# Interleaving v's rows of four heads over all partitions, and turning k behind the value products, in a chunked-attention and mixture-of-experts kernel

## The chip, the cores and the metric

The kernel runs on one core of a Trainium2 chip. The metric is the device time of one execution in microseconds (us), as the median of several runs. The core has a matrix engine (PE, with its weight loads PEld), a vector engine (DVE), a scalar engine (ACT), a general engine (POOL) and a queue engine (SP). POOL, ACT and SP also issue transfers (DMAs). Each engine works through its own instructions strictly in program order, and engines wait for each other through semaphores.

## What is computed

```python
# attention: 4 batches, 8 heads, 768 rows, 64 columns; 8 memory rows a head
for c in range(24):                       # chunks of 32 rows
    k_ctx = k[:, :, max(0, 32*c - 16):min(768, 32*c + 40)]     # 16 left, 8 right; v_ctx the same
    scores = scale * q_c @ concat(mem_k, k_ctx).T
    a = exp(scores - max); a /= a.sum()
    out[:, :, chunk c] = a @ concat(mem_v, v_ctx)
# router: each of the 3072 rows x (512 columns) goes to its 2 best of 8 experts
noisy = x @ w_gate + log1p(exp(x @ w_noise)) * noise
out[row] = sum over the two experts of weight * (relu(x @ w1[e]) @ w2[e])
```

So a chunk's 32 queries see 56 context rows and 8 memory rows, 64 in all.

## The kernel before

**Stages.** First comes the attention with the router, then the experts. The attention is a loop of 16 iterations (L579 to L638). Iteration i works on "pair" i. Pairs 2g and 2g+1 are the two halves (12 chunks each) of group g, which holds four heads of one batch; there are eight groups, two to a batch. The experts' stage begins at L655. It gathers rows by pairs of experts and runs the two products of each expert (L752, L760).

**One iteration.** The order is written out by hand (`tc.manual_schedule`), so the program text gives each engine's order. In iteration i stand, in this order:

- `PT_pe(i-1)` (L311): six transposes on PE of the probabilities P of the pair before, and `PT_dve(i-1)` (L318) which copies them to SBUF (tile PT).
- `max_dve(i)` (L299): the maximum of the scores of pair i, on DVE.
- `qkT_pe(i+2)` (L246): twelve transposes of q and twelve of k on PE for two heads. ACT copies q (L256, tile qT).
- `kT_act(i+2)` (L260): ACT copies k from PSUM into the block-diagonal buffer `kd` (`kbufs`), in two halves (L264). Before, the first half stands ahead of P's exponential and the second behind it.
- `sub_dve(i)` (L304): DVE subtracts the maximum, and ACT takes the exponential into P (L308).
- `PV_pe(i-1)` (L323): the value products on PE, six with the memory rows (L329) and 24 with the context rows of v (L333), into the single buffer `ps_o`.
- `scores_pe(i+1)` (L269): scores of the next pair on PE into the single buffer `ps_s`: the memory part (L278), which needs only q, and the chunks (L288), which need k.
- `mult_dve(i-1)` (L337): DVE divides the value products by the sums (L345, L346) into the row tile `xrow`.
- `xT_pe(i-2)` (L351): PE transposes those rows for the router, and ACT copies them (L359, tile xt).

Scores of pairs 2g and 2g+1 both need q and k of both head pairs of group g. With q and k turned two iterations ahead, an odd iteration i turns heads that the scores of pair i+1 need at once, and an even one turns heads that are needed one iteration later.

**PSUM slots.** P's transposes, q's, k's, the rows' and the router's tiles share three slots in turn (pool `psT`, L90). A transpose waits until the slot's last reader is done.

**Values.** The four heads of a group share one weight matrix PT, so v's rows lie block by block: head hd has partitions 32 hd to 32 hd + 27 (28 partitions, two rows in each), the rest of the columns is zero. The four memory partitions of each head (32 hd + 28 to 32 hd + 31) are in `memv` (L180), which also has one column of ones a head for the sums. P is written in the same order (head, row) (L307). `memory_values` (L186) copies memory rows of `mv_nat` (L150) into `memv`, on POOL, for groups 0 and 1 before the loop and for the others in iteration 2.

**Loads.** q, k and v are loaded and cast by POOL's queue, q and k one transfer a group each (L112), v one a head (L120). v has three buffers: a load waits until the products of the group before in that buffer are done. POOL also clears buffers (L139), makes constants (L212), does part of the routing and issues the loads of the first expert weights in iteration 11.

**Routing.** After the last pair of a batch, `begin_route(b)` (L541) computes the batch's logits on PE and puts the steps of `route(b)` (L375) in a list. `early_steps` and `late_steps` (L552, L557) run one entry's first and second half in each iteration: best-of comparisons (`s1m` to `s2b`), the gates (`s4`, which also sends the batch's rows to DRAM on SP's queue), the counts (`s3`, `s5`, `s5b`, `s6`) and sums (`s7`, `s8`). The last batch's steps run after the loop.

## Time and profile before

| | us |
|---|---|
| median of three runs (lowest to highest) | 341.62 (340.74 to 343.32) |
| the profiled execution's own time | 341.32 |
| its span, first to last instruction | 339.6 |
| busy in the span: PE, DVE, ACT, POOL | 294.8, 167.0, 132.1, 141.0 |

The profile is of one execution. A row of the timeline gives the start in us from the span's start, the duration, the engine, the line of the program, the operation, the tile written and the tiles read, the shape, how many instructions are merged in the row, and in brackets the idle time before it with what ended it ("issue" where nothing the profile shows was waited for). A row of a table by stretches gives the stretch, its length, the busy time of the chosen instructions with their number, the granted clock of PE, the share of the transfer engines, and the rate in GB/s of bytes written. A row of waits gives who waited for what, the total in us, the number of waits and the longest. A row of groups has the number of instructions, then the busy time in us and the mean of one in ns, then the idle time before them.

### The profile page before, as it was taken

What the parts mean: (1) busy time and instruction counts of PE and PEld (TensorE: products, weight loads), DVE (VectorE), ACT (ScalarE), POOL (GpSimd) and SP (SyncE); (2) the same over time, 40 slices, a digit from 0 to 9 for tenths busy, and PEclk for the clock granted to TensorE, in tenths of its full rate; (3) what the DMA queues carried; (4) which work ended last, traced back from release to release, by engine and by line L of the source; (5) the groups of instructions that cost most, each with busy time, mean ns of one, the idle gap of its engine ahead of it and who ended that gap; (6) DMA issues with size and microseconds to landing.
All of it is one profiled execution on the core that took longest, in us unless ns stands there. A gap on an engine that the chain in (4) does not pass through costs nothing.

```text
span 339.6 us, 8160 instructions
## 1 busy us (share of the span) xinstructions
PE 294.8 (87%) x3492; PEld 179.7 (53%) x3492; DVE 167.0 (49%) x337; ACT 132.1 (39%) x232; POOL 141.0 (42%) x183
## 2 busy tenths in 40 slices
PE   1698897878853779999999999999999999999990
PEld 1576676666642555547547545545545545545530
DVE  7776788798877653223223233334414423433440
ACT  7877886786430323333333223313133113103100
POOL 8899986274333776400061043034250222131161
PEclk9999999999995699999999999999999999999997
DMA  7999999979991379970059029419759128121021
GB/s 101 183 187 200 184 162 181 226 73 206 200 259 47 96 106 225 215 156 2 2 92 235 16 66 201 86 55 166 164 118 198 48 80 135 40 87 50 29 107 66
DMA packets 58407, 42.87 MB, mean 126 GB/s; under 512 B 32215, under 2 KB 51799, under 8 KB 58368
## 3 DMA queue, kind: packets, MB, share of 16 engines
q0 software_dynamic: 49808, 38.80, 69.0%
q1 hardware_dynamic: 8272, 3.44, 4.7%
q8 instruction: 29, 0.48, 0.5%
q10 hardware_dynamic: 288, 0.07, 0.1%
q14 instruction: 10, 0.08, 0.1%
HBM read 61.32 MB, written 10.65 MB: 212 GB/s over the span
## 4 chain that ended last, share of the span: by engine, by line
PE 70%; DMA 7%; ACT 7%; DVE 6%; POOL 4%; issue 4%; POOLq 0%; DVEq 0%; ACTq 0%
PE ps_h L752 31%; PE ps_y L760 26%; DMA kg<-in_k_dram 4%; ACT kd L264 2%; PE ps_o L329 2%; PE ps_o L333 2%; ACT xt L359 2%; DMA wgn_f<-in_moe_w_noise_dram 2%; PE p_t L697 2%; POOL out_dram L768 1%; PE ps_s L288 1%; PE p_x L357 1%; PE ps_s L779 1%; ACT P L308 1%; ACT qT L256 1%
## 5 line engine op out<-in xcount | busy, mean ns | idle before, releaser
L752 PE MATMUL ps_h<-xTb,w1t 128*128 128x512 bf16 (+3 forms) x608 | 106.3, 324 | 2.0 <-DVE xTb L698 2.0
L760 PE MATMUL ps_y<-w2t,ht 128*128 128x512 bf16 x448 | 102.0, 379 | 0.0
L752 PEld LDWEIGHTS <-w1t 128*128 128x128 bf16 x864 | 63.9, 97 | 45.2 <-DVE xTb L698 1.6
L768 POOL DMA_INDIRECT out_dram<-acc,sidx x28 | 27.9, 996 | 139.2 <-DVE acc L767 134.4
L740 DVE TENSOR_SCALAR ht<-ps_h 128x416 bf16<-128x416 f32 (+2 forms) x64 | 40.0, 625 | 72.4 <-PE ps_h L752 72.4
L738 ACT ACTIVATE ht<-ps_h 128x416 bf16<-128x416 f32 (+2 forms) x72 | 37.9, 526 | 75.4 <-PE ps_h L752 71.1
L760 PEld LDWEIGHTS <-ht 128*128 128x128 bf16 x448 | 41.8, 97 | 46.7
L764 ACT ACTIVATE acc<-ps_y,meta 128x512 f32<-128x512 f32 x28 | 19.2, 687 | 69.3 <-PE ps_y L760 56.6
L752 PE MATMUL ps_h<-xTs,w1t 128*128 128x32 bf16 x256 | 45.4, 177 | 0.2 <-DVE xTs L713 0.2
L767 DVE SCALAR_TENSOR_TENSOR acc<-ps_y,meta,acc 128x512 f32<-128x512 f32 x28 | 21.0, 751 | 37.3 <-PE ps_y L760 35.7
L688 POOL DMA_INDIRECT xl<-x_rows,gidx x28 | 29.6, 1058 | 14.3 <-issue 4.6
L120 POOL DMA_DIRECT2D vg<-in_v_dram x34 | 25.3, 750 | 4.6 <-PE ps_s L293 2.2
L698 DVE COPY xTb<-p_t 128x512 bf16<-128x512 bf16 x28 | 11.6, 422 | 29.5 <-PE p_t L697 29.4
L264 ACT COPY kd<-p_t 64x768 bf16<-64x768 bf16 x32 | 25.3, 792 | 1.2 <-PE p_t L253 0.8
L359 ACT COPY xt<-p_x 128x768 bf16<-128x768 bf16 x16 | 12.8, 799 | 15.2 <-PE p_x L357 15.2
L329 PE MATMUL ps_o<-memv,PT 128*128 128x260 bf16 x96 | 14.2, 284 | 3.5 <-DVE xrow L346 1.8
L253 PE MATMUL p_t<-identb,qg 128*64 128x128 bf16 x192 | 9.9, 246 | 7.5 <-DMA qg<-in_q_dram 6.5
L301 DVE TENSOR_REDUCE mx<-ps_s 128x12 f32<-128x768 f32 x16 | 15.2, 948 | 2.1 <-PE ps_s L293 1.2
L346 DVE TENSOR_TENSOR xrow<-ps_o,rec 128x768 bf16<-128x768 f32 x16 | 15.3, 958 | 0.6
L306 DVE TENSOR_TENSOR sd<-ps_s,mx 128x768 f32<-128x768 f32 x16 | 15.2, 949 | 0.1
L308 ACT ACTIVATE P<-sd 128x768 bf16<-128x768 f32 x16 | 13.5, 844 | 3.3 <-DVE sd L306 3.2
L256 ACT COPY qT<-p_t 128x768 bf16<-128x768 bf16 x16 | 12.8, 798 | 4.1 <-PE p_t L253 3.9
(144 smaller groups left out, 304.4 us busy)
## 6 DMA issues: line engine op xcount, KB each, us to landing
w1t<-in_moe_w_dram POOLq DMA_DIRECT2D x8, 1024.0 KB, 11.6
w2t<-in_moe_w_dram POOLq DMA_DIRECT2D x8, 1024.0 KB, 9.9
vg<-in_v_dram POOLq DMA_DIRECT2D x30, 168.0 KB, 9.2
qg<-in_q_dram POOLq DMA_DIRECT2D x7, 384.0 KB, 8.3
kg<-in_k_dram POOLq DMA_DIRECT2D x7, 384.0 KB, 10.3
x_rows<-xrow SPq DMA_DIRECT2D x3, 792.0 KB
x_rows<-xrow SPq DMA_DIRECT2D x2, 384.0 KB
xl<-x_rows,gidx POOLq DMA_INDIRECT x28, 7.2
```

The costliest lines, as they stand in the source:

```text
L120: nc.gpsimd.dma_start(out=vg[p0 + j:p0 + j + nj, c:c + n, hd, :, :].rearrange("p c e d -> p c (e d)"), in_=bass.AP(v.tensor, v.offset + (g ...
L264: nc.scalar.copy(st[n]["kT"][hs, hh, :].rearrange("d (p j) -> d p j", j=SJ), st[n]["p_k"][hs].rearrange("d j p -> d p j"))
L329: nc.tensor.matmul(out=po[:, u, :OW], lhsT=PT[:, 2 * u + e, :], rhs=memv[:, g, e, :], start=(e == 0), stop=False, skip_group_check=True)
L359: nc.scalar.copy(xt, p_x)
L688: nc.gpsimd.indirect_dma_start(out=xl, out_offset=None, in_=xd, in_offset=bass.IndirectOffsetOnAxis(ap=gidx[:, p:p + 1], axis=0), bounds_c ...
L738: nc.scalar.activation(out=dst, in_=src, func=Act.Relu)
L740: nc.vector.tensor_scalar(out=dst, in0=src, scalar1=0.0, scalar2=None, op0=Alu.max)
L752: nc.tensor.matmul(out=ps_h[:, o:o + w], lhsT=w1t[:, kp, f * 128:(f + 1) * 128], rhs=rhs(kp), start=(kp == 0 and i == 0), stop=(kp == KP - ...
L760: nc.tensor.matmul(out=ps_y, lhsT=ht[:, f, j * CAP:(j + 1) * CAP], rhs=w2t[:, f, :], start=(f == 0), stop=(f == FB - 1))
L764: nc.scalar.activation(out=accs[acc[p]], in_=ps_y, func=Act.Copy, scale=gate)
L767: nc.vector.scalar_tensor_tensor(out=a, in0=ps_y, scalar=gate, in1=a, op0=Alu.mult, op1=Alu.add)
L768: nc.gpsimd.indirect_dma_start(out=out_part[p], out_offset=bass.IndirectOffsetOnAxis(ap=sidx[:, p:p + 1], axis=0), in_=a, in_offset=None, ...
```

## The change

It has three parts. First, the order of partitions in the value products: row j of head hd moves from partition 32 hd + j to 4 j + hd. v's loads write every fourth partition; P is written as (row, head) instead of (head, row), so that the exponential writes with a step of four elements. Memory rows now lie in partitions 112 to 127. Because the four heads alternate there, `memory_values` no longer copies blocks: it multiplies the memory rows by a column `lane` that is 1 in the partitions of one head and 0 in the others. `lane` is made of an iota on POOL and two operations on DVE, and a third spreads it into the ones columns of `memv` in place of four memsets.

Second, the place of k: `qkT_pe` is called for q alone where it stood, and k's transposes with both of ACT's copies stand behind the value products, directly ahead of the next scores.

Third, the end of the loop: in the last iteration the scaling of pair 14 and the sending of its rows are moved up, the routing steps of batch 2 are divided anew, and after the loop the transposes of pair 14's rows stand before the last value products.

```diff
@@ -95,6 +95,7 @@
         groups = {}
 
         NVB, NKB = 3, 4
+        HB = 2 * GP
         turn_of = [0, 1, 0, 2, 1, 0, 2, 1]
         vbufs = [ap_.tile([128, ncnk, 2 * GP, 2, D], BF16, name=f"vg{i}", bufs=1) for i in range(NVB)]
         kbufs = [ap_.tile([128, 2, S], BF16, name=f"kd{i}", bufs=1) for i in range(NKB)]
@@ -114,11 +115,11 @@
         def load_v(g):
             vg = groups[g][2]
             for hd in range(2 * GP):
-                p0, gh = QW * hd, 2 * GP * g + hd
+                gh = 2 * GP * g + hd
 
                 def piece(c, n, j=0, nj=WP):
                     nc.gpsimd.dma_start(
-                        out=vg[p0 + j:p0 + j + nj, c:c + n, hd, :, :].rearrange("p c e d -> p c (e d)"),
+                        out=vg[hd + HB * j:hd + HB * (j + nj - 1) + 1:HB, c:c + n, hd, :, :].rearrange("p c e d -> p c (e d)"),
                         in_=bass.AP(v.tensor, v.offset + (gh * S + c * chunk + 2 * j - left_ctx) * D, [[2 * D, nj], [chunk * D, n], [1, 2 * D]]))
 
                 first, last = gh == 0, gh == B * H - 1
@@ -148,10 +149,10 @@
         zeros = ap_.tile([128, 64], BF16, name="zeros", bufs=1)
         nc.vector.memset(zeros, 0.0)
         mv_nat = ap_.tile([128, NG, 2, D], F32, name="mv_nat", bufs=1)
-        nc.vector.memset(mv_nat, 0.0)
+        nc.vector.memset(mv_nat[96:128], 0.0)
         for hd in range(2 * GP):
             nc.sync.dma_start(
-                out=mv_nat[QW * hd + WP:QW * hd + QW].rearrange("p g e d -> p g (e d)"),
+                out=mv_nat[HB * WP + hd:HB * (QW - 1) + hd + 1:HB].rearrange("p g e d -> p g (e d)"),
                 in_=bass.AP(mem_v.tensor, mem_v.offset + hd * n_mem * D, [[2 * D, n_mem // 2], [2 * GP * n_mem * D, NG], [1, 2 * D]]))
         mk_nat = ap_.tile([B * n_mem, H, D], F32, name="mk_nat", bufs=1)
         for b in range(B):
@@ -179,14 +180,18 @@
         OW = MD + 2 * GP
         memv = ap_.tile([128, NG, 2, OW], BF16, name="memv", bufs=1)
         nc.vector.memset(memv, 0.0)
-        for hd in range(2 * GP):
-            p0 = QW * hd
-            nc.vector.memset(memv[p0:p0 + QW, :, :, MD + hd:MD + hd + 1], 1.0)
+        lane_i = ap_.tile([128, HB], I32, name="lane_i", bufs=1)
+        nc.gpsimd.iota(lane_i, pattern=[[-1, HB]], base=HB, channel_multiplier=1)
+        nc.vector.tensor_scalar(out=lane_i, in0=lane_i, scalar1=HB - 1, scalar2=None, op0=Alu.bitwise_and)
+        lane = ap_.tile([128, HB], F32, name="lane", bufs=1)
+        nc.vector.tensor_scalar(out=lane, in0=lane_i, scalar1=0.0, scalar2=None, op0=Alu.is_equal)
+        mcols = memv[:, :, :, MD:].rearrange("p g e h -> p (g e) h")
+        nc.vector.tensor_copy(mcols, lane.rearrange("p (o h) -> p o h", o=1).to_broadcast(mcols.shape))
 
         def memory_values(lo, hi):
-            for hd in range(2 * GP):
-                p0 = QW * hd
-                nc.gpsimd.tensor_copy(memv[p0:p0 + QW, lo:hi, :, hd * D:hd * D + D], mv_nat[p0:p0 + QW, lo:hi])
+            for hd in range(HB):
+                nc.gpsimd.tensor_scalar(out=memv[96:128, lo:hi, :, hd * D:hd * D + D], in0=mv_nat[96:128, lo:hi],
+                                        scalar1=lane[96:128, hd:hd + 1], scalar2=None, op0=Alu.mult)
 
         zero_k(2)
         zero_v(1, 0)
@@ -243,10 +248,12 @@
         st = [dict() for _ in range(NPAIR)]
         xrows = {}
 
-        def qkT_pe(n):
+        def qkT_pe(n, names=("qT", "kT")):
             g, i = divmod(n, GP)
             qg, kg, _ = groups[g]
             for nm, src in (("qT", qg), ("kT", kg)):
+                if nm not in names:
+                    continue
                 p_t = psT.tile([128, SJ, 128], BF16, name="p_t", tag="tr")
                 for j in range(SJ):
                     for hh in range(2):
@@ -257,9 +264,9 @@
                 else:
                     st[n]["p_k"] = p_t
 
-        def kT_act(n, which=(0, 1)):
+        def kT_act(n):
             st[n]["kT"] = kbufs[n % NKB]
-            for hh in which:
+            for hh in range(2):
                 hs = slice(64 * hh, 64 * hh + 64)
                 nc.scalar.copy(st[n]["kT"][hs, hh, :].rearrange("d (p j) -> d p j", j=SJ), st[n]["p_k"][hs].rearrange("d j p -> d p j"))
 
@@ -304,8 +311,8 @@
         def sub_dve(n):
             sd = ap_.tile([128, 2, BT, CTX], F32, name="sd")
             nc.vector.tensor_tensor(out=sd, in0=st[n]["ps"], in1=bc4(st[n]["mx"], CTX), op=Alu.subtract)
-            P = ap_.tile([128, 2 * UB, 4, QW], BF16, name="P")
-            nc.scalar.activation(out=P.rearrange("p x h c -> p h x c"), in_=sd.rearrange("p x (h u) (e c) -> p (x h) (u e) c", h=2, e=2), func=Act.Exp, scale=scale)
+            P = ap_.tile([128, 2 * UB, QW, 4], BF16, name="P")
+            nc.scalar.activation(out=P.rearrange("p x c h -> p h x c"), in_=sd.rearrange("p x (h u) (e c) -> p (x h) (u e) c", h=2, e=2), func=Act.Exp, scale=scale)
             st[n]["P"] = P
 
         def PT_pe(n):
@@ -510,6 +517,8 @@
                     s1n()
                     s2d()
 
+            if b == B - 2:
+                return first_steps, ((), ()), ((s1m, s2a), (s2g, s2b, s4b, s4)), ((s3,), (s5,)), ((), (s5b, s6)), ((), (s7, s8))
             if b < B - 1:
                 return first_steps, ((), ()), ((), (s1m, s2a, s2g, s2b, s4b)), ((s3,), (s4, s5)), ((), (s5b, s6)), ((), (s7, s8))
             return first_steps, ((), (s1n, s1m, s2d, s2a, s2g, s2b, s4b, s3, s4, s5, s5b, s6, s7))
@@ -581,14 +590,12 @@
                 PT_pe(i - 1)
             max_dve(i)
             for n in ahead(i):
-                qkT_pe(n)
+                qkT_pe(n, ("qT",))
             fresh = i >= 3 and (i - 3) % HP == HP - 1
-            early_steps()
+            if i < NPAIR - 1:
+                early_steps()
             if i >= 1:
                 PT_dve(i - 1)
-            if i >= 1:
-                for n in ahead(i):
-                    kT_act(n, (0,))
             sub_dve(i)
             if i == 0:
                 load_v(1)
@@ -597,19 +604,22 @@
             if i == 1:
                 zero_k(3)
             if i == NPAIR - 1:
-                late_steps()
-            for n in ahead(i):
-                kT_act(n, (1,) if i >= 1 else (0, 1))
+                early_steps()
             if i >= 1:
                 PV_pe(i - 1)
+            for n in ahead(i):
+                qkT_pe(n, ("kT",))
+                kT_act(n)
             if i + 1 < NPAIR:
                 scores_pe(i + 1)
             if fresh:
                 begin_route((i - 3) // HP)
             if i < NPAIR - 1:
                 late_steps()
-            if 1 <= i < NPAIR - 1:
+            if i >= 1:
                 mult_dve(i - 1)
+                if i == NPAIR - 1:
+                    write_rows(B, B - 1, 0, UB, 0, XC)
             if i >= 2:
                 xT_pe(i - 2)
             if i == 1:
@@ -639,12 +649,11 @@
         n = NPAIR - 1
         PT_pe(n)
         PT_dve(n)
-        mult_dve(n - 1)
-        write_rows(B, B - 1, 0, UB, 0, XC)
+        xT_pe(n - 1)
+        late_steps()
         PV_pe(n)
         mult_dve(n)
         write_rows(B + 1, B - 1, UB, BT, 0, XC)
-        xT_pe(n - 1)
         early_steps()
         xT_pe(n)
         late_steps()
```

## The prediction

> **What bounds the kernel now.** I read the page's chain of waits first, then a table of busy time by stretches cut at each start of the maximum (L301), then one even and one odd iteration row by row, then the waits by line.
>
> ```profile
> span 339.6 us, 8160 instructions
> ```
>
> ```profile
> 114.03 4.85 PE ps_h L752 x32
> ```
>
> That is the chain's row for the first expert products. They begin at 114 us of a span of 339.6, and from there on nothing is edited. The change is worth what it moves in the attention stage and in the routing behind it. That stage is a loop of sixteen iterations; here are iterations 1 to 14, each from one maximum to the next:
>
> ```profile
> 17.70:23.14 5.44, 0.95 (x1) 1.00 1.50 190
> 23.14:27.53 4.39, 0.95 (x1) 1.00 1.58 189
> 27.53:32.69 5.16, 0.95 (x1) 1.00 1.33 206
> 32.69:37.25 4.56, 0.96 (x1) 1.00 1.75 174
> 37.25:42.09 4.84, 0.95 (x1) 1.00 1.38 192
> 42.09:46.66 4.57, 0.96 (x1) 1.00 1.57 148
> 46.66:52.21 5.55, 0.95 (x1) 1.00 1.59 176
> 52.21:58.30 6.09, 0.96 (x1) 1.00 1.63 180
> 58.30:62.98 4.68, 0.95 (x1) 1.00 1.30 236
> 62.98:68.58 5.60, 0.96 (x2) 1.00 1.82 204
> 68.58:74.13 5.55, 0.95 (x2) 1.00 0.40 35
> 74.13:79.84 5.71, 0.94 (x1) 1.00 1.48 192
> 79.84:84.50 4.66, 0.95 (x1) 1.00 1.02 190
> 84.50:89.01 4.51, 0.96 (x1) 1.00 1.12 193
> ```
>
> The second column is the iteration's length, the last the rate of the transfers. Undisturbed odd iterations (9 and 13) take 4.7 us, even ones (4 and 6) 4.6. Here are PE's rows of iterations 4 and 5 (the first is k in iteration 1) and then ACT's of iteration 5:
>
> ```profile
> 18.98 0.85 PE L253 MATMUL p_t<-identb,kg 128*64 128x128 bf16 x12
> ...
> 33.96 0.53 PE L253 MATMUL p_t<-identb,kg 128*64 128x128 bf16 x12
> 34.42 0.84 PE L329 MATMUL ps_o<-memv,PT 128*128 128x260 bf16 x6
> ...
> 38.72 0.84 PE L329 MATMUL ps_o<-memv,PT 128*128 128x260 bf16 x6
> 39.50 0.85 PE L333 MATMUL ps_o<-vg,PT 128*32 128x256 bf16 x24
> 40.28 0.31 PE L278 MATMUL ps_s<-mkd,qT 128*128 128x16 bf16 x6
> 41.46 0.20 PE L288 MATMUL ps_s<-kd,qT 128*32 128x80 bf16 x1 [0.88 <-issue]
> ```
>
> ```profile
> 38.07 0.80 ACT L256 COPY qT<-p_t 128x768 bf16<-128x768 bf16 x1
> 38.77 0.79 ACT L264 COPY kd<-p_t 64x768 bf16<-64x768 bf16 x1
> 39.56 0.84 ACT L308 ACTIVATE P<-sd 128x768 bf16<-128x768 f32 x1
> 40.43 0.79 ACT L264 COPY kd<-p_t 64x768 bf16<-64x768 bf16 x1
> ```
>
> ```profile
> PE ps_s L288 <- ACT kd L264: 3.4, 5, 1.0
> ```
>
> Two things are to be seen. In an odd iteration the next scores need the k that is turned in that same iteration, and PE waits for ACT's second copy of it: it ends at 40.43 + 0.79 = 41.22, 3.97 us after the maximum began, and PE stands for 0.88. That is the end of an odd iteration. In an even one the next scores need no new k. There PE is late in front of the value products: they start at 34.42 - 32.69 = 1.73 us, behind k's transposes, and in iteration 5, where PT (the copy of the transposed P) came last, at 38.72 - 37.25 = 1.47.
>
> **The change part by part.**
>
> k turned behind the value products. Odd iteration: the value products start 1.47 us after the maximum; PE's next work comes 40.28 - 38.72 = 1.56 later; that is now the twelve transposes of k, 0.53; then both copies of k on ACT, with the pitch of the rows above, 38.77 - 38.07 = 0.70 and 0.79; then the scores up to the next maximum, 42.09 - 41.46 = 0.63. Sum 5.68, say 5.7 with the steps between engines. P's exponential is out of the way: it ended at 40.40, 3.15 after the maximum, and k's first copy can begin at 3.6. Against the table: iteration 5 +0.87, 9 +1.03, 13 +1.05. Iterations 1, 3, 7 and 11 hold another wait already and are at 5.16 to 5.55; 5.7 would add 0.27, 0.55, 0.16 and 0.16. In 1 (PE there takes 0.85 for twelve transposes) and 7 (P's transposes come late behind the router's logits) the value products start some 0.6 later than 1.47, so I take 0.9 and 0.8. Odd iterations: +5.4.
>
> Even iteration: k's transposes no longer stand before the value products. Iterations 4 and 6 gain 1.73 - 1.47 = 0.26. In 8 and 10, where routing steps make PE later still, the whole pitch of the twelve, 34.42 - 33.96 = 0.46. Iteration 2 starts nearly on time, 12 waits for the routing's one-hot, 14 turns no k. Even iterations: -1.4.
>
> The tail. The value products of the last pair now wait less:
>
> ```profile
> 95.30 0.84 PE L329 MATMUL ps_o<-memv,PT 128*128 128x260 bf16 x6 [1.78 <-DVE xrow L346]
> ...
> 99.67 0.41 PE L368 MATMUL ps_l<-wgn,xt 128*128 128x16 bf16 x10 [0.56 <-ACT xt L359]
> ```
>
> The scaling of pair 14 (L345, L346) is moved into iteration 15, ahead of the router's count of batch 2, and PE's 1.78 of waiting falls to about 1. What is late next is DVE: count, mask and gates of batch 2 (four small operations more) now stand ahead of the last scaling. I estimate that 0.8 of wait less gives 0.6 at the last logits (99.67). The bounds are 0 and 1.78. On SP the rows of pair 14 go out earlier, and batch 2's rows with their gates now stand ahead of the last pair's; nothing is behind these in the queue but batch 3's gates, and the gathers need them only when batch 3 has been routed.
>
> P in the order (row, head). ACT writes the same 768 numbers with a step of four. No row has such a write; k's copies read with a step of 128 elements and take 0.79 for 768, and q's 0.80, so steps of that size cost nothing there. I take 0. The upper end is twice 0.84, the lower nothing, since the count of elements stays. The transposes of P read the same contiguous 128 columns.
>
> Memory rows by a mask. On POOL eight casts become eight multiplications with a scalar column.
>
> ```profile
> L189 POOL CAST memv<-mv_nat 32x768 bf16<-32x768 f32 x4 | 3.3, 818 | 0.2
> L476 POOL TENSOR_SCALAR ohp<-oh,part 128x168 bf16<-128x168 bf16 x4 | 2.9, 715 | 0.0
> ```
>
> The lower end is the cast itself; the upper is L476 stretched by the number of elements, 0.715 x 768/168 = 3.3 for the large and 1.1 for the small ones, some 12 us more on POOL. I take the nearest row, the cast of the same shapes, plus L476's excess of about 0.4 over a cast of its size, 8 x 0.4 = 3.2 us. POOL is full until then:
>
> ```profile
> 39.15 5.96 POOL L120 DMA_DIRECT2D vg<-in_v_dram  x8 [0.51 <-issue]
> 45.10 0.78 POOL L112 DMA_DIRECT2D qg<-in_q_dram  x1
> 45.86 0.76 POOL L112 DMA_DIRECT2D kg<-in_k_dram  x1
> 47.91 0.29 POOL L395 TENSOR_TENSOR nl<-ns,nz_all 128x48 f32<-128x48 f32 x1 [1.29 <-ACT lg L387]
> ```
>
> Queued behind these are the loads of k and q, the constants for DVE in iteration 5, v's eight loads at 39.15 and the routing step at 47.91. The pauses of 0.51 and 1.29 and the 1.8 us by which iterations 1 to 6 have become longer (0.9 + 0.55 - 0.26 + 0.87 - 0.26) make a cover of 3.6, above 3.2. I charge 0.3, for loads of v that land just late. On DVE three short operations for the mask replace four short memsets, and wait for one iota on POOL; mv_nat is cleared in 32 partitions instead of 128 at the same length of rows. I take 0 for the start, with some 0.3 either way; if the iota came late, all of DVE's filling of buffers and the first maximum would stand behind it.
>
> v over all partitions. The same number of loads, packets and bytes. One wait in the trace is for v:
>
> ```profile
> PE ps_o L333 <- DMA vg<-in_v_dram: 0.6, 1, 0.6
> ```
>
> It lies in iteration 11, which is at 5.55 and will be 5.7 for k's sake, so I take 0; the bounds are -0.6 and the same upward. The rate in the table is 174 to 206 GB/s in most early stretches, whichever of q, k and v is on the way, so v's layout does not show as a limit. [...]
>
> **Sum.** The profiled execution took 341.32, its span 339.6; the median of the three runs is 341.62, 0.3 above. 341.3 + 5.4 - 1.4 - 0.6 + 0.3 = 345.0.
>
> **The rivals.**
>
> *Covered.* Only iterations 5, 9 and 13 pay; in 1, 3, 7 and 11 the waits that are there already cover all of it. For it speaks that these four are near 5.7 today. 341.3 + 0.87 + 1.03 + 1.05 - 1.4 - 0.6 = 342.3.
>
> *Faster.* The place is the wait of the scores for k's second copy. If k's copies, with P's exponential no longer between them, ended by 3.97 us after the maximum as now, odd iterations would gain PE's earlier start too: thirteen iterations (1 to 13) at 0.26 are 3.4, with the tail 4.0: 337.3. It decides at that 3.97; my rows put the end at 1.47 + 1.56 + 0.53 + 0.70 + 0.79 = 5.05, over 1 us too late, which speaks against.
>
> *POOL becomes the bound.* With 12 us more, v's loads of 39.15 come some 8 us beyond the cover of 3.6; about 7 of that reaches the value products: 345.0 + 7 = 352. It decides from 3.6 us on POOL. Against it speaks the cast's 0.818 for the same shapes.
>
> *The step of four costs.* P at 1.68 instead of 0.84 ends at 4.0 instead of 3.15, and k's copies start 0.4 later in seven odd iterations (2.8); in the six that follow an even one ACT is also behind with q (0.35 each, 2.1): 345 + 4.9 = 350.
>
> *v lands sooner.* If rows spread over all partitions speed up v's loads, the 0.6 of iteration 11 goes before k's copies count: 345.0 - 0.6 = 344.4. The steady rate in the table speaks against it. [...]
>
> **How the numbers follow.** Forecast 0.5, with 343.4 to 347.5 as its own range; covered 0.2; faster 0.07; POOL 0.08; step of four 0.1; v sooner 0.05. The predicted time is 345.0. Leaving out the faster case and POOL's (0.15), the range is 341.0 to 350.5. A measurement of this kernel tells about 1% from no change, 338.2 to 345.0. The forecast lies on that upper edge, and its own range reaches further up than down: 0.3 of its 0.5 is above, with POOL and the step 0.18 more, 0.48. Faster is 0.07, and 0.45 remains within.
>
> **What would show it.** In the profile after, iterations 5, 9 and 13 at 5.7 with PE's scores waiting over 1 us for k's copy; iterations 4 and 6 at 4.3; the value products 1.47 after the maximum; P still 0.84; the masked multiplications under 1.3 us for the large ones; nothing waiting for v or POOL in iterations 5 to 7; last logits 0.6 sooner after the last maximum than 99.67 - 89.01 = 10.66. The prediction is wrong if odd iterations stay near 4.7, or if an exponential or POOL row doubles.

## The result, and the profile after

The changed kernel takes 355.62 us (median of four runs, 354.69 to 356.79), the kernel before, run beside it, 342.4 (340.74 to 343.32). The ratio is 1.0394, its 95% interval 1.0336 to 1.0451: 13.2 us slower. The forecast was 345.0 with a range to 350.5, so the time lies above the range. The profiled execution took 356.79. Medians here are over all executions of a kernel, while ratios leave out executions in a slower state, so a ratio need not be the quotient of two medians.

Three views answer to those shown of before. First the span, from the page, and the first expert products, from the chain of waits:

```profile
span 355.1 us, 8141 instructions
```

```profile
129.34 5.35 PE ps_h L761 x32
```

They begin 15.3 us later than before (114.03), and the span is 15.5 longer. Everything was lost ahead of the experts. Next the table by stretches, iterations 1 to 14, each from one maximum (now L308) to the next; the second column is the length, then come the busy times of PE, PEld, DVE, ACT and POOL, and third from the end stands the clock that was granted to TensorE (PE):

```profile
17.69:26.01 8.32, 6.20 (x97) 4.20 (x98) 4.33 (x7) 6.42 (x7) 8.02 (x10) 1.00 1.36 161
26.01:31.67 5.66, 5.02 (x96) 3.36 (x95) 3.47 (x5) 3.46 (x3) 3.79 (x5) 0.70 1.25 162
31.67:38.47 6.80, 4.45 (x103) 3.38 (x103) 3.48 (x6) 5.71 (x7) 6.56 (x6) 1.00 1.52 190
38.47:42.82 4.35, 4.04 (x102) 3.15 (x101) 3.43 (x6) 3.62 (x4) 4.28 (x2) 1.00 0.48 49
42.82:49.60 6.78, 4.26 (x103) 3.32 (x103) 3.95 (x11) 6.11 (x7) 6.04 (x12) 1.00 0.84 120
49.60:53.94 4.34, 4.04 (x104) 3.15 (x103) 3.42 (x6) 3.62 (x4) 4.34 (x7) 1.00 1.13 107
53.94:61.35 7.41, 5.09 (x126) 3.96 (x126) 5.67 (x11) 6.92 (x11) 7.24 (x12) 0.99 1.57 159
61.35:67.07 5.72, 5.72 (x108) 4.58 (x108) 4.80 (x11) 4.17 (x4) 3.53 (x6) 0.72 1.55 184
67.07:73.45 6.38, 4.33 (x105) 3.32 (x105) 4.36 (x12) 5.71 (x7) 2.59 (x4) 1.00 1.32 235
73.45:79.77 6.32, 5.77 (x116) 4.29 (x115) 3.60 (x6) 4.15 (x4) 0.00 (x0) 0.73 1.68 167
79.77:86.67 6.90, 5.00 (x127) 3.96 (x127) 5.19 (x11) 6.41 (x11) 4.85 (x10) 1.00 0.18 17
86.67:91.71 5.04, 4.37 (x109) 3.57 (x108) 4.72 (x12) 4.28 (x4) 4.95 (x8) 1.00 1.46 180
91.71:98.10 6.39, 4.34 (x105) 3.33 (x104) 4.36 (x13) 5.71 (x7) 0.43 (x1) 1.00 1.06 214
98.10:104.12 6.02, 5.37 (x98) 3.80 (x97) 3.58 (x7) 2.73 (x2) 0.00 (x0) 0.55 1.19 190
```

Odd iterations take 6.4 to 8.3, where 5.7 was forecast (6.3 in 1 and 7). Iterations 4 and 6 take 4.35 and 4.34, as forecast (4.3). Iterations 2, 8, 10 and 14 stand out: their clock is 0.55 to 0.73, which no iteration before had. By the starts of the maximum the odd ones lost 13.1 together, the even ones 2.0.

Now iteration 5 in the timeline, PE's rows and then ACT's:

```profile
44.24 0.53 PE L260 MATMUL p_t<-identb,qg 128*64 128x128 bf16 x12 [0.68 <-ACT kd L271]
44.69 0.84 PE L336 MATMUL ps_o<-memv,PT 128*128 128x260 bf16 x6
...
46.25 0.53 PE L260 MATMUL p_t<-identb,kg 128*64 128x128 bf16 x12
...
49.03 0.25 PE L295 MATMUL ps_s<-kd,qT 128*32 128x80 bf16 x4 [1.84 <-ACT kd L271]
```

```profile
45.60 1.96 ACT L315 ACTIVATE P<-sd 128x768 bf16<-128x768 f32 x1
47.28 1.70 ACT L271 COPY kd<-p_t 64x768 bf16<-64x768 bf16 x2
```

The exponential takes 1.96 where it took 0.84. It ends at 47.56, 4.7 after the maximum; k's transposes are done at 46.78 and wait behind it on ACT. The two copies end at 48.98, and the scores of the next pair wait 1.84 for them. The late copies of the iteration before also hold a PSUM slot, so q's transposes wait 0.68 and the value products start 1.87 after the maximum, not 1.47. The groups by form show the exponential and POOL's multiplications (count, busy us and ns of one), the waits by line the scores' wait (in total, times, longest):

```profile
L315 ACT ACTIVATE P<-sd 128x768 bf16<-128x768 f32 x16 | 31.0, 1938 | 5.7 <-DVE sd L313 5.7
L193 POOL TENSOR_SCALAR memv<-mv_nat,lane 32x768 bf16<-32x768 f32 x4 | 8.8, 2208 | 0.3
L193 POOL TENSOR_SCALAR memv<-mv_nat,lane 32x256 bf16<-32x256 f32 x4 | 3.7, 930 | 0.3
```

```profile
PE ps_s L295 <- ACT kd L271: 13.3, 8, 1.8
```

So both rows that the prediction named as signs of being wrong have more than doubled: P from 0.844 to 1.938, the large memory rows from 0.818 to 2.208. Last, one of the clock's falls: PE's rows at the end of iteration 1 and in iteration 2, and the table in two stretches of 3.4 us around 27.0:

```profile
25.43 0.25 PE L295 MATMUL ps_s<-kd,qT 128*32 128x80 bf16 x4 [1.28 <-ACT kd L271]
...
27.49 1.48 PE L336 MATMUL ps_o<-memv,PT 128*128 128x260 bf16 x6 [0.64 <-DVE PT L327]
28.90 1.48 PE L340 MATMUL ps_o<-vg,PT 128*32 128x256 bf16 x24
```

```profile
23.60:27.00 3.40, 1.97 (x56) 1.43 (x52) 1.64 (x3) 1.64 (x3) 3.40 (x3) 1.00 1.54 139
27.00:30.40 3.40, 2.91 (x32) 1.66 (x34) 1.30 (x2) 2.66 (x2) 1.83 (x3) 0.51 1.16 157
```

PE was busy for 1.97 of the 3.4 us ahead; then the clock is at half for 3.4 us, and the value products take 1.48 + 1.48 in place of 0.84 + 0.85. Read in slices of 0.2 us, this fall and those of iterations 8 and 10 each add up to 3.41 us at half clock, and the one that begins in iteration 14 to 6.82, twice that. In the 3.4 us ahead of the falls of iterations 8, 10 and 14 PE was busy for 1.62, 1.59 and 1.56. In the kernel before, no stretch of 3.4 us in iterations 2 to 14 has less than 2.16.

### The profile page after: what moved, and what is told of

It reads as the page before. It is cut to its first block, busy times and chain, and to the rows that moved or that the text cites. A ratio compares the mean times of both kernels' runs of the same rounds, so it can differ in the third digit from the quotient of the medians.

```text
span 355.1 us, 8141 instructions
## 1 busy us (share of the span) xinstructions
PE 301.3 (85%) x3474; PEld 183.8 (52%) x3492; DVE 168.5 (47%) x336; ACT 149.6 (42%) x232; POOL 149.6 (42%) x184
## 2 busy tenths in 40 slices
DMA packets 58407, 42.87 MB, mean 121 GB/s; under 512 B 32215, under 2 KB 51799, under 8 KB 58368
## 4 chain that ended last, share of the span: by engine, by line
PE 67%; ACT 10%; DVE 9%; issue 4%; DMA 4%; POOL 4%; POOLq 0%; DVEq 0%; ACTq 0%
PE ps_h L761 30%; PE ps_y L769 25%; ACT P L315 4%; ACT kd L271 4%; DMA vg<-in_v_dram 2%; PE ps_o L336 2%; PE ps_o L340 2%; PE p_t L260 2%; PE p_t L706 2%; DVE vg L137 2%; POOL out_dram L777 1%; DVE sd L313 1%; PE ps_s L788 1%; DVE mx L308 1%; POOL vg L121 1%
## 5 line engine op out<-in xcount | busy, mean ns | idle before, releaser
L769 PE MATMUL ps_y<-w2t,ht 128*128 128x512 bf16 x430 | 100.5, 379 | 1.0 <-issue 0.2
L315 ACT ACTIVATE P<-sd 128x768 bf16<-128x768 f32 x16 | 31.0, 1938 | 5.7 <-DVE sd L313 5.7
L271 ACT COPY kd<-p_t 64x768 bf16<-64x768 bf16 x32 | 26.3, 822 | 3.1 <-PE p_t L260 2.8
L295 PE MATMUL ps_s<-kd,qT 128*32 128x112 bf16 (+2 forms) x384 | 10.9, 230 | 13.3 <-ACT kd L271 13.3
L308 DVE TENSOR_REDUCE mx<-ps_s 128x12 f32<-128x768 f32 x16 | 15.3, 953 | 11.6 <-PE ps_s L295 10.5
L336 PE MATMUL ps_o<-memv,PT 128*128 128x260 bf16 x96 | 16.3, 316 | 3.0 <-DVE PT L327 2.9
L340 PE MATMUL ps_o<-vg,PT 128*32 128x256 bf16 x384 | 16.0, 308 | 0.0
L353 DVE TENSOR_TENSOR xrow<-ps_o,rec 128x768 bf16<-128x768 f32 x16 | 15.3, 957 | 0.6
```

Source lines behind the costliest of these rows:

```text
L271: nc.scalar.copy(st[n]["kT"][hs, hh, :].rearrange("d (p j) -> d p j", j=SJ), st[n]["p_k"][hs].rearrange("d j p -> d p j"))
L315: nc.scalar.activation(out=P.rearrange("p x c h -> p h x c"), in_=sd.rearrange("p x (h u) (e c) -> p (x h) (u e) c", h=2, e=2), func=Act.E ...
L336: nc.tensor.matmul(out=po[:, u, :OW], lhsT=PT[:, 2 * u + e, :], rhs=memv[:, g, e, :], start=(e == 0), stop=False, skip_group_check=True)
L340: nc.tensor.matmul(out=po[32 * r:32 * r + 32, u, :MD], lhsT=PT[:, 2 * u + e, 32 * r:32 * r + 32], rhs=vg[:, CB * half + x, :, e, :], start ...
L769: nc.tensor.matmul(out=ps_y, lhsT=ht[:, f, j * CAP:(j + 1) * CAP], rhs=w2t[:, f, :], start=(f == 0), stop=(f == FB - 1))
```

## The experiments

The theories after the result were these. W: ACT's write with a step of four costs 1.1 us in each iteration. M: POOL's multiplications are too long to be hidden. K: k behind the value products is dearer than the sum said. H: TensorE's clock falls after iterations in which PE waits, and that is a loss of its own. They overlap, so each part was done alone and undone alone. Kernels ran on several chips, on which the kernel before took 341.95 to 345.95 (medians); ratios to it are what is compared. The edits shown are shortened; `...` and missing arguments stand for what is left out.

### The order alone, the layout alone

Both are the kernel before with one part of the change's diff. order_only has the edits of `qkT_pe`, `kT_act`, `route`, the loop and the tail, and none of the others; layout_only has those of `load_v`, `mv_nat`, `memv`, `memory_values` and `P`:

```diff
 order_only
-def kT_act(n, which=(0, 1)):
+def kT_act(n):
...
 layout_only
-P = ap_.tile([128, 2 * UB, 4, QW], BF16, name="P")
+P = ap_.tile([128, 2 * UB, QW, 4], BF16, name="P")
...
```

> Only the new order of the work: k behind the value products, the scaling of pair 14 moved into iteration 15, the routing steps of batch 2 shifted; P, v and the memory rows as in the kernel before. Theory W (the exponential's write with a step of four costs 1.1 us each time, and the rest of the prediction's sum stands): P's exponential back at 0.84 us, odd iterations at 5.7, even ones at 4.3 to 4.6, time 344.7. Theory K (turning k behind the value products is itself dearer than the sum says, through TensorE's clock: its long waits in odd iterations are followed by a granted clock near 0.7 in even ones, whatever P costs): iterations 2, 8, 10 or 14 show a clock under 0.8 again, time 348 or more. Theory M (the masked multiplications on POOL delay v): says nothing here; 344.7 too.

> Only the new layout: v's rows interleaved, P written with a step of four, the memory rows by a mask; the order of the work as in the kernel before. Theory W: the exponential at 1.94 us stands between the two copies of k, so the second copy ends 1.09 later in odd iterations (5.06 instead of 3.97 us after the maximum), 7 x 1.09 = 7.6; in even iterations ACT has 0.80 + 0.79 + 1.94 + 0.79 + about 0.8 = 5.1 us of work against a length of 4.6, some 0.5 x 6 = 3; time 352. Theory K: the order of k is what costs, so about 343 to 345. Theory M: POOL's 7.6 us more delays v by some 4 beyond the cover, 345 to 347, with waits of the value products for vg in iterations 5 to 9.

order_only: 348.68, ratio 1.017 (1.0074 to 1.0266). layout_only: 355.03, ratio 1.0369 (1.0279 to 1.0459). Each is slower by itself, and together they are no slower than the layout alone. Iterations 3 and 4 of order_only, and its value products of pair 14 in iteration 15:

```profile
29.13:34.96 5.83, 4.33 (x102) 3.32 (x101) 3.48 (x6) 4.72 (x7) 5.66 (x8) 1.00 1.46 195
34.96:39.31 4.35, 4.05 (x102) 3.17 (x101) 3.43 (x5) 3.19 (x4) 4.24 (x5) 1.00 1.55 176
```

```profile
97.03 1.48 PE L331 MATMUL ps_o<-memv,PT 128*128 128x260 bf16 x6 [0.65 <-DVE PT L322]
98.43 1.48 PE L335 MATMUL ps_o<-vg,PT 128*32 128x256 bf16 x24
```

With the exponential at 0.84 odd iterations that nothing else disturbs are at 5.83 (5.7 forecast), and all of 1 to 14 keep clock 1.00, so in this trace the order alone brings no fall of the clock there. It comes in iteration 15, where the clock is 0.51 from 97.00 to 100.40 and the value products of pair 14 take 1.48 + 1.48 (those of pair 15 take 0.84 + 0.85 again).

### The exponential's write

The step was moved in two ways that keep the order of P.

```diff
 after_p_read (ACT reads with a step)
-out=P.rearrange("p x c h -> p h x c"), in_=sd.rearrange("p x (h u) (e c) -> p (x h) (u e) c", h=2, e=2)
+out=P.rearrange("p x c h -> p (x c) h"), in_=sd.rearrange("p x (h u) c -> p (u c) (x h)", h=2)
 after_p_sub (DVE writes with a step)
-sd = ap_.tile([128, 2, BT, CTX], F32, name="sd")
-nc.vector.tensor_tensor(out=sd, ...)
+sd = ap_.tile([128, UB, CTX, 4], F32, name="sd")
+nc.vector.tensor_tensor(out=sd.rearrange("p u k (x h) -> p x h u k", x=2), ...)
```

> The changed kernel whole, but the exponential writes P in one run of addresses and reads the differences with a step instead (the four heads of one column lie 192 numbers of 4 bytes apart). Same numbers, same place in P. Theory W: if reading with a step is free, P is back at 0.84 us and the time at 344.7 plus at most 4 for POOL: 345 to 349; if reading costs as writing does, 355 again and P near 1.9. Theory K: P shorter but the time still over 350, with the clock falls. Theory M: over 350 also.

> The changed kernel whole, but the change of order is made one step earlier: DVE's subtraction writes the differences with a step of four 4-byte numbers, and the exponential reads and writes runs of addresses. Theory W: the exponential is back at 0.84; if DVE's write pays what ACT's paid, the subtraction goes from 0.95 to about 2.0 and the time stays near 355; if it pays nothing, the time is that of the new order alone, 348.7, plus what POOL's masked multiplications then let show (the reading form had POOL in its chain), 349 to 352. Theory H: long stalls gone, clock at 1.00 in the loop. The rival that the order of the rows or v's landing itself is dear: 353 or more with the exponential at 0.84 and the subtraction at 0.95.

The reading form: 353.72, ratio 1.036 (1.0269 to 1.0452). The subtracting form: 356.22, ratio 1.0333 (1.0266 to 1.0399). The step is dear wherever it is put:

```profile
L315 ACT ACTIVATE P<-sd 128x768 bf16<-128x768 f32 x16 | 24.9, 1557 | 6.2 <-DVE sd L313 6.1
```

```profile
L313 DVE TENSOR_TENSOR sd<-ps_s,mx 128x768 f32<-128x768 f32 x16 | 24.6, 1538 | 0.0
```

The first row is the reading form's exponential, the second the subtracting form's subtraction (0.95 before), which puts the exponential back at 0.844. Neither tells W from M by its time, since POOL's work was still in both. So the price was measured by itself, with trial operations between the routing and the experts.

```diff
...
+for sp in (1, 2, 3, 4):
+    nc.scalar.activation(out=spaced(t_w, sp), in_=t_in[:, :192], func=Act.Exp)
+for sp in (4, 8):
+    nc.scalar.activation(out=spaced(t_w, sp, 96), in_=t_in[:, :96], func=Act.Exp)
...
+nc.gpsimd.tensor_scalar(out=tg, in0=t_in[96:128], scalar1=t_one[96:128, 0:1], scalar2=None, op0=Alu.mult)
+nc.gpsimd.tensor_scalar(out=tg, in0=t_in[96:128], scalar1=1.0, scalar2=None, op0=Alu.mult)
+nc.gpsimd.tensor_tensor(out=tg, in0=t_in[96:128], in1=t_f[96:128], op=Alu.mult)
+nc.gpsimd.tensor_copy(tg, t_in[96:128])
```

> The kernel before with a row of trial operations put between the routing and the expert products: ACT's exponential of 192 numbers written to bf16 with steps of 1, 2, 3 and 4 (96 numbers with steps of 4 and 8), to 4-byte numbers with steps 1, 2 and 4, and read from 4-byte numbers with steps 2 and 4; DVE's copy written with steps 1 and 4; POOL's 32 x 768 with a column as factor, with a constant as factor, with two tiles, and as a cast. Their results go nowhere. Theory W (a write with a step costs by the step's bytes): by the exponential at 844 and 1938 ns for 768 numbers the step of four bf16 costs 1.4 ns a number, so 192 numbers take about 0.27 us more at step 4 and at step 3, and a step of 2 may be free; a reading step costs 0.9 ns a number by the 1557 of the reading form. The rival (not the step but the short runs of 32 numbers, or the order of the loops, is what costs): 192 numbers take the same at all steps. The masked 32 x 768 on POOL: 2208 again with a column; if the column is what costs, a constant gives 820 as the cast does.

ACT's six writes one by one (lowest, median and highest ns, start), in the order of the code:

```profile
L669 ACT ACTIVATE P<-sd x1: 363/363/363, 110.5 to 110.5; 128x192 bf16<-128x192 f32 x1
L669 ACT ACTIVATE P<-sd x1: 416/416/416, 110.9 to 110.9; 128x192 bf16<-128x192 f32 x1
L669 ACT ACTIVATE P<-sd x1: 521/521/521, 111.3 to 111.3; 128x192 bf16<-128x192 f32 x1
L669 ACT ACTIVATE P<-sd x1: 627/627/627, 111.9 to 111.9; 128x192 bf16<-128x192 f32 x1
L671 ACT ACTIVATE P<-sd x1: 415/415/415, 112.5 to 112.5; 128x96 bf16<-128x96 f32 x1
L671 ACT ACTIVATE P<-sd x1: 626/626/626, 113.0 to 113.0; 128x96 bf16<-128x96 f32 x1
```

From step 1, 768 numbers at 844 and 192 at 363 give 0.835 ns a number and 203 ns fixed. Less these 203, a number costs 1.11, 1.66 and 2.21 ns at steps 2, 3 and 4, and 4.41 at step 8: some 0.55 ns times the step. It is the step that costs, not the run length: 768 x 2.21 + 203 gives 1900, near the 1938 seen. Each trial ran once. Reading 192 numbers of 4 bytes, ACT took 353 ns at a step of 2 and 538 at 4; DVE's copy of 192 to 2-byte numbers took 260 at a step of 1 and 382 at 4. (The trials with 4-byte results took 594, 373 and 537 ns at steps 1, 2 and 4; I have no reading of them.) On POOL:

```profile
116.36 2.24 POOL L679 TENSOR_SCALAR P<-sd,t_one 32x768 bf16<-32x768 f32 x1 [9.14 <-DVE void L687]
118.69 2.13 POOL L680 TENSOR_SCALAR P<-sd 32x768 bf16<-32x768 f32 x1
120.90 1.80 POOL L681 TENSOR_TENSOR P<-sd 32x768 bf16<-32x768 f32 x1
122.77 0.82 POOL L682 CAST P<-sd 32x768 bf16<-32x768 f32 x1
```

It is not the column as factor that is dear: each of the three multiplications takes twice the cast or more.

### The write and POOL's multiplications, undone one by one

```diff
 after_m_cast
-nc.gpsimd.tensor_scalar(out=memv[96:128, ...], in0=mv_nat[96:128, lo:hi], scalar1=lane[96:128, hd:hd + 1], ...)
+nc.gpsimd.tensor_copy(memv[96:128, ...], mv_nat[96:128, lo:hi])
 after_flat
-P = ap_.tile([128, 2 * UB, QW, 4], BF16, name="P")
+P = ap_.tile([128, 2 * UB, 4, QW], BF16, name="P")
-out=P.rearrange("p x c h -> p h x c")
+out=P.rearrange("p x h c -> p h x c")
```

after_flat_cast has both edits, layout_flat is layout_only with the edit of after_flat, and after_read_cast has those of after_p_read and after_m_cast.

> The changed kernel, but the memory rows are cast without the mask (all four heads' columns get the row's values, so the memory part of the output is not the reference's): POOL's eight operations are casts of the same shapes again, 7.6 us less on POOL. Theory W: POOL is covered for the most part, 354 to 356. Theory M: the delay goes, 348 to 351, and the waits of transposes and value products for the loads go with it. Theory K: 355.

> The changed kernel whole, but the exponential writes P head by head, in runs of 32, as the kernel before did, while v, the memory rows and the order are the new ones: the value products mix the heads and the output is not the reference's. Theory W: the exponential at 0.84, odd iterations at 5.83 as in order_only, ratio to the kernel before 1.017 (order_only's) plus what POOL's 7.6 us then cost, at most 4 us: 1.017 to 1.03. If the new layout costs beyond the write and POOL: over 1.03.

> As after_flat, with POOL's unmasked casts in place of the multiplications. All that is left of the change is its order and where v's rows lie. Theory W: order_only again, ratio 1.017. If v over all partitions lands sooner and that helps: under 1.01; if it hurts: over 1.025.

> The new layout of v and of the memory rows, in the kernel before's order, with P written head by head (heads are mixed, the output is not the reference's). Theory W: the exponential at 0.84, so iterations 9 and 13 at 4.7 as before; ratio 1.000 to 1.005 if POOL's 7.6 us are covered, 1.005 to 1.015 with waits for vg in iterations 5 to 8 if not. If v's layout costs or gives something by itself: iterations 9 and 13 away from 4.7, or under 0.99.

> The reading form of the exponential (1.56 us) and, beside it, POOL's casts without the mask in place of the multiplications (the memory part of the output is not the reference's). Theory M2 (POOL's 7.6 us are hidden only while ACT is slower; in the reading form they were in the chain): 2 to 4 us faster than after_p_read's 353.7, iterations 5 and 7 shorter than its 7.32 and 8.71, and the value products' wait of 1.8 for vg gone. Theory W alone: 353 to 354 as before. Measured against order_only (348.7), what remains above it is the exponential's 0.71 in odd iterations and the clock's falls.

| the changed kernel with | ratio (interval) | odd, even iterations 1 to 14, us |
|---|---|---|
| neither (after_flat_cast) | 1.0205 (1.0168 to 1.0242) | 43.0, 33.0 |
| POOL's multiplications alone (after_flat) | 1.032 (1.0267 to 1.0374) | 48.0, 35.8 |
| the dear write alone (after_m_cast) | 1.0423 (1.0339 to 1.0506) | 48.0, 38.4 |
| both (the change) | 1.0394 (1.0336 to 1.0451) | 49.0, 37.5 |
| order_only, for comparison | 1.017 (1.0074 to 1.0266) | 43.3, 33.7 |
| the kernel before | 1 | 35.9, 35.4 |

(The sums are worked out from the starts of the maximum in each trace.) Either cost alone makes the kernel slower. POOL's multiplications on top of the dear write are not seen. The write on top of POOL's multiplications lengthens the loop by 2.6 us, while the intervals of the ratios overlap; in the order of before the same step, from layout_flat (1.0214) to layout_only (1.0369), is clear of the intervals. after_flat and after_flat_cast ran on the same chip, 353.34 and 348.26: without the dear write POOL's multiplications cost 5.1 us. In the changed kernel no cost of theirs shows: they end at 42.87 there, and the value products of iteration 5, which need them, start at 44.69 without waiting for them, because a loop that ACT slows down asks for its values later:

```profile
33.81 9.06 POOL L193 TENSOR_SCALAR memv<-mv_nat,lane 32x768 bf16<-32x768 f32 x4
```

layout_flat, ratio 1.0214 (1.0178 to 1.025), shows where they strike, in iteration 5 (9.79 us), PE's row and then POOL's:

```profile
41.45 1.40 PE L334 MATMUL ps_o<-memv,PT 128*128 128x260 bf16 x6 [2.99 <-POOL memv L193]
```

```profile
32.35 9.05 POOL L193 TENSOR_SCALAR memv<-mv_nat,lane 32x768 bf16<-32x768 f32 x4
```

The value products wait 2.99 for the memory rows themselves, and v's loads stand behind them on POOL. after_read_cast, ratio 1.0314 (1.0228 to 1.0401), agrees in its trace (iterations 5 and 7 at 6.12 and 6.76, after 7.32 and 8.71 in the reading form), but the time's gain over the reading form is within the intervals. And v's interleaving by itself: after_flat_cast has it and order_only has not, and their intervals cover each other.

### TensorE's clock

```diff
...
+for f in range(filler):
+    nc.tensor.matmul(out=ps[:, f % GP, BT * CTX:512], lhsT=identb, rhs=onesb, start=True, stop=True)
...
-scores_pe(i + 1)
+scores_pe(i + 1, 18 if i % 2 else 0)
```

> The changed kernel with 18 extra matrix products of 128 x 128 in each odd iteration, ahead of the scores that wait for k; they go into columns that no one reads, and take about 1 us of a wait of 1.3 to 2. Theory H (part of the loss is TensorE's clock, which falls to 0.55 to 0.73 in iterations 2, 8, 10 and 14 because TensorE stood for 2 us or more in the odd iteration ahead): the clock stays at 1.00 in most of them, even iterations lose their 2 to 3.5 us over before, 350 to 353. Theory W alone (the exponential sets the length, the clock only follows): the clock may rise but the time stays at 355 to 357.

354.48, ratio 1.0286 (1.0212 to 1.036). The clock is 1.00 in all of iterations 1 to 14. (Pauses of 2 us, as the expectation has them, were not there to be filled: the scores' longest wait in the changed kernel is 1.8.) Iterations 2, 8, 10 and 14:

```profile
26.01:30.35 4.34, 3.71 (x96) 2.81 (x95) 3.42 (x6) 2.82 (x3) 3.78 (x5) 1.00 1.11 130
...
60.05:64.81 4.76, 4.57 (x113) 3.71 (x112) 4.59 (x11) 4.03 (x4) 3.19 (x5) 1.00 1.48 188
...
71.19:76.08 4.89, 4.34 (x116) 3.55 (x115) 3.60 (x6) 3.56 (x4) 0.00 (x0) 1.00 1.83 200
...
94.89:99.40 4.51, 3.86 (x109) 3.15 (x108) 3.58 (x7) 2.75 (x2) 0.00 (x0) 1.00 1.18 198
```

They were 5.66, 5.72, 6.32 and 6.02: 5.2 us gained, and 0.5 paid in the odd ones. More work on PE made the stage shorter, so H is shown for the loop: the falls come from PE's waiting, and without them it is 4.7 us shorter, of the 15.1 that it had lost. The first expert products begin 5.2 us sooner, at 124.13 instead of 129.34. The time in us shows less of it, for the two did not run side by side: the experts' stage, which no edit touches, took 229.4 us in this trace and 225.8 in that of the changed kernel, and the kernel before took 344.74 beside the one and 342.4 beside the other. The gain by the ratios, 1.1% of 342 or 3.7 us, has intervals that just overlap.

The tail and the pauses ahead of the experts were tried on the kernel before.

```diff
 tail_only: of the change's diff, route's shifted steps and their calls in iteration 15, mult_dve and write_rows of pair 14, the last lines
 tail_warm: tail_only, and
 begin_route(B - 1)
...
+for f in range(44):
+    nc.tensor.matmul(out=idle[:, f % GP, :128], lhsT=identb, rhs=onesb, start=True, stop=True)
 late_steps()
...
 for p in plan[0]:
     gather(p)
...
+for f in range(30):
+    nc.tensor.matmul(out=idle[:, 128 * (f % 4):128 * (f % 4) + 128], lhsT=identb, rhs=onesb, start=True, stop=True)
```

> The kernel before with the change's tail alone: pair 14 scaled in iteration 15, the routing steps of batch 2 shifted. The prediction: 0.6 faster, 341.3 to 341.4. Theory H: the same if the clock stays at 1.00 through iteration 15, and up to 2.5 more if a pause lets it fall there, as in order_only, whose last value products took 1.48. The rival (DVE's added steps ahead of the last scaling cost what the shorter wait gives): 341.9 to 342.5.

> The kernel before with the change's tail (tail_only, 1.000) and extra products on TensorE that no one reads: 44 while it waits 3.4 us for the routing of batch 3, 30 while it waits 2.4 us for the gathered rows. Theory H: the granted clock, 0.50 there in the kernel before, is higher when the expert products start; the first 32 of them take 3.7 instead of 4.85 us and the transposes ahead of them 0.4 instead of 0.6: 1.2 to 2 us faster, ratio 0.994 to 0.997. The rival (the start hangs on the gathers alone and the later start of nothing else follows): 1.000.

tail_only: ratio 1.0004 (0.9958 to 1.0051); its last logits come 10.17 after the last maximum, against 10.66. tail_warm: 340.88 against 342.27, ratio 0.9967 (0.9934 to 1.0000). The first expert products in its trace:

```profile
112.36 3.65 PE L759 MATMUL ps_h<-xTb,w1t 128*128 128x256 bf16 x32 [0.52 <-DVE xTb L705]
```

They take 3.65 at clock 1.00, where in the kernel before they take 4.85 at 0.74. This is the only version that came out below the kernel before, by 0.3%, with an interval that ends at no difference.

### The wait for k itself

```diff
 k_even: before, and
+behind = i % 2 == 0 and i >= 1
...
-    qkT_pe(n)
+    qkT_pe(n, ("qT",) if behind else ("qT", "kT"))
...
 PV_pe(i - 1)
+for n in ahead(i) if behind else ():
+    qkT_pe(n, ("kT",))
+    kT_act(n)
 la3 (from before) and order_la3 (from order_only)
-return [i + 2] if i + 2 < NPAIR else []
+return [2, 3] if i == 0 else [i + 3] if i + 3 < NPAIR else []
...
```

> The kernel before, with k turned behind the value products in even iterations alone, where the next scores need no new k; odd iterations, the layout, the routing steps and the tail as before. The prediction's sum: even iterations gain 1.4, measured 1.7 in the run with the whole new order, odd ones and the tail stay: 340.2 to 340.6. Theory H: nothing to do here, the clock stays 1.00. The rival (an even iteration's gain is only a debt of the odd one that follows, whose work then lies later): 342 to 343.

> The kernel before with q and k turned three pairs ahead instead of two, nothing else. The wait of the odd iterations' scores for k's second copy (3.4 us in five) goes, 1 us is added in iteration 0: 339 to 341. The rival (transfers of q and k set the pace of the stage, since they land 8 to 10 us after their issue): 342 or more, with waits for kg in iterations 1 to 6.

> The new order alone (k behind the value products, as in the run order_only; layout as in the kernel before), but q and k are turned three pairs ahead instead of two, two pairs in iteration 0, so that no iteration's scores need a k that is turned in it. The prediction's reason for the odd iterations (the scores wait for k turned in the same iteration) holds if odd iterations fall from 5.83 to 4.35 as the even ones have: seven times 1.5 less, about 10 us less than order_only, 338 to 341 with 1 us more in iteration 0. The rival (something else in the new order lengthens odd iterations): they stay at 5.8 and the time at 347 to 350. Theory H (clock): iterations 12 to 15 without long pauses keep 1.00. A risk for both: the loads of q and k are needed an iteration sooner, and a wait for them may take the place of the one for k.

k_even: 349.19, ratio 1.01 (1.0033 to 1.0167). Even iterations are at 4.35, but 3, 5 and 13 rise to 5.45, 5.39 and 5.28 (5.16, 4.84 and 4.66 before): the rival holds, the copies that an even iteration puts off stand ahead of the odd one's on ACT. In all, the odd ones lost 3.0 us, and the even ones gained 1.8 without iteration 12. The rest of the loss lies elsewhere: iteration 12 waits 1.82 us for POOL's one-hot, falls to clock 0.78 and takes 7.72 instead of 5.71, and the last logits come 13.06 after the last maximum instead of 10.66, with pair 14's value products at 1.48 + 1.48. la3: ratio 1.0155 (1.0086 to 1.0224), with iterations 3, 9 and 13 at 4.30 and 1 and 7 at 9.91 and 8.41. order_la3: 348.11, ratio 1.011 (1.0043 to 1.0176). Its iterations 3 and 9, and the waits of iterations 1, 7 and 12:

```profile
30.25:34.63 4.38, 4.16 (x103) 3.22 (x102) 3.46 (x7) 3.91 (x6) 4.25 (x6) 1.00 1.44 195
...
61.19:65.57 4.38, 4.16 (x105) 3.23 (x105) 4.35 (x12) 3.96 (x6) 2.62 (x4) 1.00 1.50 250
```

```profile
21.16 0.85 PE L256 MATMUL p_t<-identb,qg 128*64 128x128 bf16 x12 [2.21 <-DMA qg<-in_q_dram]
...
53.38 0.85 PE L336 MATMUL ps_o<-vg,PT 128*32 128x256 bf16 x24 [2.23 <-DMA vg<-in_v_dram]
...
79.31 0.30 PE L443 MATMUL ps_r<-oh,upper 128*128 128x168 bf16 x1 [2.23 <-POOL oh L436]
```

Without k in the way an undisturbed odd iteration takes 4.38 instead of 5.83: the wait for k turned in the same iteration is what the odd iterations pay. But a faster loop meets its loads and POOL: three waits of 2.2 us, each with a fall of the clock (0.77 in iteration 1, 0.95 in 7 and 0.76 in 8, 0.77 in 12), take the gain back (iterations 1, 7 and 12 at 7.50, 7.46 and 7.55).

## Why the prediction was wrong

- **P with a step of four: 0 in the sum.** This step failed. It measured 1.1 us of ACT in each iteration. Against after_flat_cast, which has neither cost, the write alone is worth 1.0423 - 1.0205, about 7.5 us (after_m_cast), and the write with POOL's multiplications 1.0394 - 1.0205, 6.5 us; the two differ by less than their intervals, and the clock's falls (to 0.54 in iteration 14 of the one, to 0.55 in that of the other) are a part of both. The rows that it rested on were k's and q's copies (0.79 and 0.80), which read PSUM with a step of 128 elements; beside the 1.938 of the write they were no evidence for a write to SBUF. The upper end that was set beside it, twice 0.84, was too low as well: four times the step costs 2.21/0.835 = 2.6 times as much for each number. The rival "the step of four costs" had the mechanism (P behind k's transposes, k's copies late in odd iterations) and a time of 350, which is short by the size of the write, by the clock and by what the order itself cost beyond 345.0.
- **TensorE's clock: not in the sum.** The clock was 1.00 in all fourteen rows quoted, and nothing asked what makes it so. In the change it fell, to 0.55 to 0.73 in iterations 2, 8, 10 and 14, after PE had been busy for only 1.56 to 1.97 of 3.4 us, and 2.0 us lost in even iterations that were to gain 1.4 are its work: without the falls they took 32.2, 3.2 less than before.
- **Odd iterations, k's order: 5.4.** The mechanism was right and is shown by order_la3. Undisturbed ones measured 5.83 against 5.68, all seven 7.4. The largest miss is iteration 1, +1.66 against +0.9. There the value products take 1.48 + 1.48 in order_only, where they took 1.39 + 0.85. In the eight traces read there (before, after, order_only, layout_only, after_p_read, after_m_cast, order_la3, la3) PE's rows are that slow at first (twelve transposes take 0.85 there and 0.53 later), until some 21 to 29 us into the span. The order does not decide that: with k's transposes where before has them, these products take 1.48 + 1.23 in layout_only and 1.48 + 1.48 in la3. The table has the clock at 1.00 there, so the trace does not say why, and part of this miss may be chance. The next is iteration 11, +0.85 against +0.16: at 6.40 it came out like iteration 7 (6.39), for which the sum had +0.8; PE is busy for 5.00 and 4.99 in the two, 4.33 in iteration 3.
- **Even iterations: -1.4.** In order_only they gained 1.7, as forecast. What the sum did not see is that the gain is a debt to the odd iteration behind it, which k_even showed.
- **The tail: -0.6.** By itself it gave 0.5 at the last logits. In order_only the last logits came 0.97 later, not sooner, with pair 14's value products at half the clock (0.51), and in the changed kernel 0.27 later.
- **Memory rows on POOL: 3.2 us more, 0.3 charged.** The size failed: 7.6 more, between the two ends, by 2.208 against the 1.2 taken. The cover of 3.6 was then too small, as the POOL rival said: 5.1 us show where the write is cheap. In the changed kernel they do not show, because ACT's exponential gave POOL time. That the charge of 0.3 came out about right was luck.
- **v over all partitions: 0.** Right, as far as the intervals of after_flat_cast and order_only tell. The 0.6 of the rival "v lands sooner" was not seen in the time: v's loads took 7.3 us from issue to landing (median) in the changed kernel, and 7.1 in order_only, where v lies as before.

In all, the order with v's layout cost 7.0 us (2.05%) where 3.4 was forecast, and the write with POOL's multiplications another 6.5 where 0.3 was.

## What to carry to other kernels

Before a layout is interleaved, measure what the writing engine pays for the step, on the same memory and in the same direction; a cheap read elsewhere is no evidence (k's copies read with a step of 128 in 0.79 us, the write with a step of four took 1.94). Where PE's clock falls with its waiting, as in this loop, a wait that is added can cost twice, once as itself (the scores' 1.28 in iteration 1) and once in the half clock that follows (iteration 2 at 5.66, 4.34 without the fall), and useless products in the wait can be cheaper than the pause (5.2 us gained here, 0.5 paid). Undo each part alone and both together: two costs on different engines that overlap hide one another, and removing one of them can show little or nothing (here 1.0394 with both, 1.0423 and 1.032 with one).

## What the runs showed of the chip

- ACT's write of 2-byte numbers with a step took 1.11, 1.66, 2.21 and 4.41 ns a number at steps 2, 3, 4 and 8, about 0.55 ns times the step, beside some 200 ns fixed (price, each trial once; the 1938 of the exponential agrees). At a step of four 192 numbers took 627 ns, at a step of one 363.
- TensorE's clock fell to half for about 3.4 us after 3.4 us in which PE was busy for 1.97, with no pause over 1.28; the falls in the changed kernel's loop last 3.41 us or twice that. What decides a fall is open: order_only has pauses of 1.28 in odd iterations, and 3.5 us from 22.5 on with PE busy for 1.84, and keeps its clock at 1.00 there, while ahead of its fall in iteration 15 PE was busy for 2.17 of 3.4.
- POOL's multiplication of 32 x 768 numbers took 2.13 us with a constant, 2.24 with a column (2.208 in the loop) and 1.80 with two tiles, and the cast 0.82.
